# One inverse of softmax sums for two pairs of heads in the first batch of an attention and gated-MLP kernel

## The chip, the core and the metric

The kernel runs on one core of one Trainium2 chip. The metric is the time of one execution on the device, in microseconds (us); lower is better. The engines are named as in the profile: PE multiplies matrices (PEld is its weight load), DVE, ACT and POOL work on tiles elementwise, SP issues most of the DMAs. Each engine takes its instructions in the order in which the program lists them for that engine.

## The reference

Windowed attention with a bias that falls with distance, and then a gated MLP whose gate mixes along the sequence. Cut to what is computed:

```python
# attention: B, H, S, D = 8, 8, 576, 64; window 128
scores = q @ k.T / sqrt(D) + slope[h] * -abs(i - j)   # where 0 <= i - j < 128, else -1e9
attn = exp(scores - max(scores))
attn = attn / (sum(attn) + 1e-9)
x = attn @ v                                          # heads side by side: (8, 576, 512)
# gated MLP
h = relu(x @ w_in); u, v = h[..., :512], h[..., 512:]
v_n = (v - mean(v)) / sqrt(var(v) + 1e-6)
out = (u * (w_spatial @ v_n + b_spatial)) @ w_out
```

## The kernel before, in words

The work of a batch is attention for four pairs of heads, and then the units of the MLP: v (lines 696 to 722, and 724 to 750 for the rest of 64 rows), u (752 to 768), s (770 to 798) and o (800 to 822). Queries go in five tiles of 128 rows, t = 0 to 4, the last of 64. A tile of queries sees at most 256 keys.

Most batches go through `scores` and `attention`: the probabilities are split into two half-precision parts (line 576 on ACT, line 581 on DVE) and turned by a DMA transpose. The whole first batch, and pair 0 of the second, go through `raw_tile` instead (line 427), one call for each tile t and pair p. One call plans these steps, for both heads j of the pair:

- line 441, PE: the scores of both heads, into two of four PSUM buffers "s".
- line 447, DVE, once per head: bias and mask are added, the row minimum of the negated scores is kept in `rstat`, column NM, and the result goes to `prob[j]`, slot p.
- line 452, ACT, once per head: exp, with the sum of the row kept in `rstat`, column SM.
- lines 456 and 457, DVE: 1e-9 is added to the two sums, and the inverse is taken. Both instructions work on 128 x 2 elements: one column per head. The rest of this document calls the two together one inverse.
- lines 460 or 461: the probabilities are multiplied by the inverse, on ACT or on DVE, once per head.
- line 470, PE: the probabilities are transposed into a PSUM buffer "m" (of two, which the weight splits and the MLP units also use, in a fixed sequence).
- line 278: they are copied to SBUF (`pq`), on ACT or DVE; line 488, PE: they multiply v, into a buffer "x"; lines 278 and 496: the result is split into a high and a low part, `xt`, which the MLP reads.

`rstat` has eight rows of eight columns; tile t of pair p has row p + 4 (t mod 2), so that the rows of neighbouring tiles of t don't meet. A slot of `prob` is taken again by tile t + 1 of its pair, after the transposes of tile t. The calls stand in `first(t)` (line 844): the four pairs of one t, then the split of one quarter of the u weights (`split_w64`, lines 290 to 339, mostly DVE). `gated(0, ...)` calls `first(0)` and `first(1)`, and then `first(i + 2)` ahead of each v unit i.

What sets the order of the work: nothing is emitted at once. `plan.add` notes an operation with its engine, a cost in ns, a due time and the parts of buffers it reads and writes; `plan.order` (line 93) then plays the whole program through with these costs and emits, on each engine, the ready operation with the earliest due time. An operation added with `plan.either` goes to the engine on which it would end first, so the choice between lines 460 and 461 hangs on the plan. An inverse costs 190 in the plan, is due 900 after its tile, and a tile of pair p is due 1500 after that of pair p - 1. Which instruction stands behind which on DVE and ACT is so decided before the program runs, by modelled times:

```python
raw_tile(0, p, t, *loads[p], x0[p], p, 2000 + t * 6500 + p * 1500)   # line 846
plan.add("DVE", 190, due + 900, f, [(rstat, row)], [(rstat, row)])   # line 458
```

Of the kernel before, what the change touches and what calls it, by code (L numbers as in the profile page):

```python
# [16 lines left out]
ALU = mybir.AluOpType  # L17
# [123 lines left out]
def attn_gmlp_kernel(ctx, tc, qk, v, w_in, w_spT, b_sp, w_out, outT):  # L141
# [3 lines left out]
    nc = tc.nc  # L145
    B, H, D, _, S = qk.shape
    P = 2 * D
    NP = H // 2
    NQ = (S + P - 1) // P
# [29 lines left out]
    plan = Plan()  # L179
# [4 lines left out]
    def fixed(shape, dtype, name):  # L184
        t = const.tile(shape, dtype, name=name)
        return Buf(lambda: t)

    def dve(n, fast=False):
        return 75 + n / (1.92 if fast else 0.96)

    def act(n, pointers=0):
        return 95 + n / 1.2 + 93 * pointers
# [18 lines left out]
    r1 = fixed([P, S], F32R, "r1")  # L211
# [4 lines left out]
    prob = [fixed([P, NB * P], F32, f"prob{j}") for j in range(2)]  # L216
# [3 lines left out]
    rstat = fixed([P, 8, 8], F32, "rstat")  # L220

    def parts(b, a, z, step=P, key=()):

        return [(b, (*key, k)) for k in range(a // step, -(-z // step))]
# [122 lines left out]
    def win_weights(half, c, due, st):  # L347
        cs = slice(half * DH, (half + 1) * DH)
        split_w64((st, DH), (win, (half, c)), [plan.buf(work, "gs", 5, [P, DH], F32) for _ in range(2)],
                  lambda: win()[:, c, 0, cs], lambda: win()[:, c, 1, cs], due, WPE[half])  # L350
# [61 lines left out]
    def load(b, p, due, pieces, qtag=("qkraw", 3), vtag=("vraw", 3)):  # L412

        raw = plan.buf(work, *qtag, [P, 2, S], F32)
        vr = plan.buf(work, *vtag, [P, NQ, P], F32)
        src = qk[b, 2 * p:2 * p + 2].rearrange("h d a s -> (h d) a s")
        t0 = 0
        for i, t1 in enumerate(pieces):
            cs, ts_ = slice(t0 * P, min(S, t1 * P)), slice(t0, t1)
            plan.add("SP", dma(P * 2 * (cs.stop - cs.start) * 4), due[i], lambda cs=cs: nc.sync.dma_start(raw()[:, :, cs], src[:, :, cs]),  # L420
                     (), [(raw, t) for t in range(t0, t1)])
            plan.add("SP", dma(P * (t1 - t0) * P * 4), due[i] + 500, lambda ts_=ts_: nc.sync.dma_start(vr()[:, ts_], v[b, p][:, ts_]),
                     (), [(vr, t) for t in range(t0, t1)])
            t0 = t1
        return raw, vr

    def raw_tile(b, p, t, raw, vr, xt, slot, due):

        m, k0, k1 = min(P, S - t * P), max(0, (t - 1) * P), min(S, (t + 1) * P)
        n, c0 = k1 - k0, P if t == 0 else 0  # L430
        blocks = [(k, min(P, k1 - k)) for k in range(k0, k1, P)]
        row, NM, SM, TM, RC = (slot + 4 * (t % 2)) % 8, 0, 2, 4, 6
        st = lambda k, j: rstat()[:m, row, k + j:k + j + 1]
        sc = [plan.buf(ps, "s", 4, [P, 2, 2 * P], F32) for _ in range(2)]
        pr = [lambda j=j: prob[j]()[:m, slot * 2 * P:slot * 2 * P + n] for j in range(2)]
        cols = [parts(prob[j], slot * 2 * P, slot * 2 * P + n) for j in range(2)]

        def f():
            for j in range(2):
                rows = slice(j * D, (j + 1) * D)  # L440
                nc.tensor.matmul(sc[j]()[:m, 0, :n], raw()[rows, 0, t * P:t * P + m], raw()[rows, 1, k0:k1], start=True, stop=True)
        plan.add("PE", SWITCH // 2 + pe(*[4 * n]), due, f, [(raw, k) for k in range(k0 // P, t + 1)], [(sc[j], 0) for j in range(2)])
        for j in range(2):
            h = 2 * p + j

            def f(j=j, h=h):
                nc.vector.tensor_tensor_reduce(pr[j](), sc[j]()[:m, 0, :n], tabs[h]()[:m, c0:c0 + n], -0.125, 3e38,
                                               ALU.add, ALU.min, st(NM, j))
            plan.add("DVE", dve(n), due + 300, f, [(sc[j], 0), (tabs[h], 0)], cols[j] + [(rstat, row)])

            def f(j=j):
                nc.scalar.activation(pr[j](), pr[j](), AF.Exp, bias=st(NM, j), scale=-1.0, accum_out=st(SM, j))
            plan.add("ACT", act(n, 2), due + 600, f, cols[j] + [(rstat, row)], cols[j] + [(rstat, row)])

        def f():
            nc.vector.tensor_scalar(rstat()[:m, row, TM:TM + 2], rstat()[:m, row, SM:SM + 2], 1e-9, None, ALU.add)
            nc.vector.reciprocal(rstat()[:m, row, RC:RC + 2], rstat()[:m, row, TM:TM + 2])
        plan.add("DVE", 190, due + 900, f, [(rstat, row)], [(rstat, row)])
        for j in range(2):
            plan.either([("ACT", act(n, 1), lambda j=j: nc.scalar.activation(pr[j](), pr[j](), AF.Copy, scale=st(RC, j))),  # L460
                         ("DVE", dve(n, True), lambda j=j: nc.vector.tensor_scalar(pr[j](), pr[j](), st(RC, j), None, ALU.mult))],
# [83 lines left out]
    def scores(b, p):  # L545

        due = FIRST + b * PERIOD - LEAD - (NP - 1 - p) * PERIOD // 4
        st = stat[p % 2]
        SM, NM, RC, TM = range(4)
        raw, vr = load(b, p, [due - 12000], [NQ])  # L550
        RAWS, VRS = [(raw, t) for t in range(NQ)], [(vr, t) for t in range(NQ)]
        if (b, p) in RAW:
            xt = plan.buf(work, "xt", 6, [P, 2 * S + R], F32R)
            for t in range(NQ):
                raw_tile(b, p, t, raw, vr, xt, t % 4, due - 6000 + t * 1500)
            return lambda: xt
        for g, banks in enumerate((BANKS,) if b >= WHOLE else (BANKS[:2], ((BANKS[2][0], ("s", 4)),))):
            products(p, due, st, raw, RAWS, g, banks)
        pts = []
        for j in range(2):  # L560
            d = due + j * 1500

            def f(j=j):
                nc.vector.tensor_scalar(st()[:, TM, j, :NQ], st()[:, SM, j, :NQ], 1.0 / PSC, 1e-9 / PSC, ALU.mult, ALU.add)  # L564
            plan.add("DVE", 100, d, f, [(st, (SM, j, t)) for t in range(NQ)], [(st, (TM, j))])

            def f(j=j):
                nc.vector.reciprocal(st()[:, RC, j, :NQ], st()[:, TM, j, :NQ])  # L568
            plan.add("DVE", 120, d, f, [(st, (TM, j))], [(st, (RC, j))])
            for t in range(NQ):  # L570
                m = min(P, S - t * P)
                n = P if t == 0 else m + P
                cs = slice(OFF[t], OFF[t] + n)

                def f(j=j, t=t, m=m, cs=cs):
                    nc.scalar.activation(pq[j]()[:m, 0, cs], prob[j]()[:m, cs], AF.Copy, scale=st()[:m, RC, j, t:t + 1])  # L576
                cols, out = parts(prob[j], cs.start, cs.stop), [parts(pq[j], a * NB * P + cs.start, a * NB * P + cs.stop) for a in range(2)]
                plan.add("ACT", act(n, 1), d + 100 + t * 250, f, cols + [(st, (RC, j))], out[0])

                def f(j=j, t=t, m=m, cs=cs):  # L580
                    nc.vector.scalar_tensor_tensor(pq[j]()[:m, 1, cs], prob[j]()[:m, cs], st()[:m, RC, j, t:t + 1],  # L581
                                                   pq[j]()[:m, 0, cs], ALU.mult, ALU.subtract)
                plan.add("DVE", dve(n), d + 110 + t * 250, f, cols + [(st, (RC, j))] + out[0], out[1])
            pts.append(plan.buf(work, "pt", 3, [P, 2 * NB, P], F16))

            def f(j=j):
                nc.sync.dma_start_transpose(out=pts[j](), in_=pq[j]().rearrange("p a b -> p (a b)"))
            plan.add("SP", 3400, d + 1500, f, parts(pq[j], 0, 2 * NB * P), [(pts[j], 0)])

        return lambda: attention(p, due, vr, VRS, pts)  # L590
# [94 lines left out]
    def gated(b, xt, first=lambda t: None):  # L685
# [134 lines left out]
        for i in range(2):  # L820
            first(i)
        for i, t in enumerate(range(NQ) if b == 0 else VORDER):
            first(i + 2)
            v_rem() if t == NQ - 1 else v_unit(t)
# [16 lines left out]
    x0 = [plan.buf(work, "xt", 6, [P, 2 * S + R], F32R) for _ in range(NP)]  # L841
    loads = [load(0, p, [-50000 + 1000 * p, -20000 + 1000 * p], [2, NQ], *where[p]) for p in range(NP)]

    def first(t):
        for p in range(NP) if t < NQ else ():
            raw_tile(0, p, t, *loads[p], x0[p], p, 2000 + t * 6500 + p * 1500)
        if 0 <= t - 2 < NC_:
            c = t - 2
            win_weights(0, c, UDUE[c], w_u[c])
# [3 lines left out]
    def rest(b, p, f):  # L853
        xts.append(f())
        if p == NP - 1:
            gated(b, [xts.pop(0) for _ in range(NP)])

    gated(0, x0, first)
    todo = []
    for b in range(1, B):  # L860
        for p in range(NP):
            if b == 1 and (b, p) not in RAW and (b, p - 1) in RAW:
                clear()
            todo.append((b, p, scores(b, p)))
            if len(todo) > AHEAD:
                rest(*todo.pop(0))
# [35 lines left out]
```

## Time and profile before

| what | value |
|---|---|
| median of 3 runs | 634.85 us (632.7 to 635.41) |
| profiled execution | 634.76 us, of which 633.0 us are its span from first to last instruction |
| PE busy | 594.8 us (94% of the span) |
| PEld busy | 522.8 us (83%) |
| DVE busy | 537.0 us (85%), 1969 instructions |
| ACT busy | 425.7 us (67%) |
| POOL busy | 30.1 us (5%) |
| DMA | mean 127 GB/s |
| granted clock of PE, mean | 0.983 of full speed |

The shares are means over the whole span. The work of the first batch lies in the first 72 us, so the stretches of that time count here, each with the busy time of every engine and the granted clock of PE (1.00 is 2.4 GHz, 0.50 is 1.2 GHz). In lists of groups the columns are line, engine and operation, tiles, shapes and count, then busy us and mean ns of one, and the idle time of the engine ahead of them with what ended it. In timelines they are start, length, instruction, count, and in brackets the idle time ahead of it with its releaser. Neighbouring instructions of an engine overlap at their ends: what one costs its engine is the distance from its start to the next start.

### The profile page before, as it was taken

How to read it: one execution, taken by the hardware profiler on the slowest of the kernel's cores; microseconds unless marked ns; L12 is line 12 of the kernel's file. 1: busy time of each engine (PE TensorE's matmuls, PEld its weight loads, DVE VectorE, ACT ScalarE, POOL GpSimd, SP SyncE). 2: the span in 40 equal slices, each digit the busy share in tenths (PEclk: the TensorE clock that was granted, in tenths of full speed). 3: DMA queues.
4: the chain of work that ended last, by engine and by line, in shares of the span. 5: the costliest groups of instructions: out<-in, count | busy, mean ns of one | idle time of the engine just before them, and what ended most of it. 6: DMA issues, size and time to landing. Idle time of an engine off the chain costs nothing. (4 is left out here: it accounts for less than half of the span.)

```text
span 633.0 us, 14919 instructions
## 1 busy us (share of the span) xinstructions
PE 594.8 (94%) x5388; PEld 522.8 (83%) x5388; DVE 537.0 (85%) x1969; ACT 425.7 (67%) x1308; POOL 30.1 (5%) x53
## 2 busy tenths in 40 slices
PE   4888899799999899999999999999999999999997
PEld 2455578588789887999789988999899889998997
DVE  7999888889988979978899999999999899983632
ACT  4698675787767867858587676976597568752211
POOL 1000010000010001000110001000200010000100
PEclk9989799979999999999999999999999999999999
DMA  7902123498744873667636863597656761761001
GB/s 263 342 21 92 55 67 100 127 204 195 155 70 109 202 163 98 135 143 164 119 104 125 191 166 94 116 189 179 137 115 145 175 127 27 106 137 38 0 20 57
DMA packets 153613, 80.27 MB, mean 127 GB/s; under 512 B 132930, under 2 KB 144194, under 8 KB 153540
## 3 DMA queue, kind: packets, MB, share of 16 engines
q1 hardware_dynamic: 153540, 79.32, 53.4%
q8 instruction: 42, 0.69, 0.4%
q14 instruction: 31, 0.25, 0.1%
HBM read 37.13 MB, written 9.44 MB: 74 GB/s over the span
## 5 line engine op out<-in xcount | busy, mean ns | idle before, releaser
L541 ACT ACTIVATE prob<-prob,stat 128x256 f32<-128x256 f32 (+2 forms) x270 | 125.9, 469 | 36.7 <-DVE stat L535 36.5
L781 PE MATMUL m<-wsp,vn 128*128 128x288 f32 x768 | 122.0, 298 | 2.8 <-DVE o L278 1.6
L760 PE MATMUL m<-xt,win 128*128 128x288 f32 x768 | 111.3, 298 | 4.2 <-DVE u L283 2.3
L807 PE MATMUL m<-gs,wout 128*128 128x288 f32 x768 | 113.0, 302 | 0.7 <-DVE o L278 0.4
L781 PEld LDWEIGHTS m<-wsp,vn 128*128 128x128 f32 x768 | 107.2, 188 | 6.4 <-issue 2.0
L760 PEld LDWEIGHTS m<-xt,win 128*128 128x128 f32 x768 | 104.0, 188 | 9.0 <-DVE u L283 4.1
L807 PEld LDWEIGHTS m<-gs,wout 128*128 128x128 f32 x768 | 105.0, 191 | 6.2 <-DVE gs L795 1.8
L576 ACT ACTIVATE pq<-prob,stat 128x128 f16<-128x128 f32 x270 | 105.4, 468 | 5.0 <-DVE stat L568 1.6
L581 DVE SCALAR_TENSOR_TENSOR pq<-prob,stat,pq 128x128 f16<-128x128 f32 x270 | 105.0, 435 | 1.7 <-ACT pq L576 1.0
L708 PE MATMUL m<-win,xt 128*128 128x512 f32 x384 | 92.8, 396 | 1.7 <-ACT o L278 0.6
L708 PEld LDWEIGHTS m<-win,xt 128*128 128x128 f32 x384 | 72.2, 190 | 18.8 <-ACT vt L282 0.9
L535 DVE CUSTOM_DVE_ANT_0 prob<-s,tab 128x256 f32<-128x256 f32 (+2 forms) x222 | 74.8, 379 | 0.9 <-PE s L524 0.2
L789 DVE TENSOR_TENSOR u<-m,u 128x288 f32<-128x288 f32 x64 | 28.8, 451 | 28.8 <-PE m L781 28.5
L678 POOL TENSOR_TENSOR st<-st,nhalf 128x1 f32<-128x1 f32 (+1 forms) x40 | 26.1, 653 | 546.5 <-DVE st L674 526.4
L541 ACT ACTIVATION_READ_ACCUMULATOR prob<-prob,stat 128x1 f32 (+1 forms) x270 | 51.3, 190 | 0.0
L524 PE MATMUL s<-qkraw 64*64 64x192 f32 (+2 forms) x876 | 42.6, 317 | 5.0 <-DVE stat L535 5.0
L643 PE MATMUL x<-pt,vh 128*64 128x32 f16 (+6 forms) x756 | 42.4, 229 | 1.7 <-DMA pt<-pq 1.7
L524 PEld LDWEIGHTS s<-qkraw 64*64 64x64 f32 x876 | 31.4, 136 | 11.7 <-DVE stat L535 7.0
L643 PEld LDWEIGHTS <-vh 128*64 128x64 f16 x756 | 32.6, 110 | 7.0 <-issue 6.6
L669 DVE BATCH_NORM_STATS2 st<-vt 128x6 f32<-128x512 f32 (+1 forms) x40 | 27.5, 688 | 12.8 <-ACT vt L282 12.7
L278 ACT COPY o<-m 128x288 f32<-128x288 f32 x35 | 13.8, 393 | 35.9 <-PE m L807 25.7
L282 ACT ACTIVATE vt<-m 128x512 f32<-128x512 f32 x32 | 19.0, 595 | 26.7 <-DVE st L673 16.8
(133 smaller groups left out, 850.1 us busy)
## 6 DMA issues: line engine op xcount, KB each, us to landing
qkraw<-in_qk_dram SPq DMA_DIRECT2D x28, 576.0 KB, 4.1
out_dram<-o SPq DMA_DIRECT2D x64, 144.0 KB, 2.3
vraw<-in_v_dram SPq DMA_DIRECT2D x28, 320.0 KB, 3.1
vn<-in_w_in_dram SPq DMA_DIRECT2D x6, 512.0 KB, 6.5
pt<-in_w_out_dram SPq DMA_DIRECT2D x4, 512.0 KB, 4.2
gs<-in_w_spT_dram SPq DMA_DIRECT2D x4, 288.0 KB, 5.2
xt<-in_w_in_dram SPq DMA_DIRECT2D x2, 512.0 KB, 6.4
qkraw<-in_qk_dram SPq DMA_DIRECT2D x3, 320.0 KB, 8.7
```

Source lines behind the costliest of these rows:

```text
L524: nc.tensor.matmul(sc[k][j]()[out, i, a - k0:z - k0], raw()[rows, 0, q:q + D], raw()[rows, 1, a:z], start=True, stop=True, skip_group_chec ...
L535: nc.vector.tensor_tensor_reduce(pt(), sc()[:m, i, :n], tabs[h]()[:m, c0:c0 + n], -0.125, 3e38, ALU.add, ALU.min, st()[:m, NM, j, t:t + 1])
L541: nc.scalar.activation(pt(), pt(), AF.Exp, bias=st()[:m, NM, j, t:t + 1], scale=-1.0, accum_out=st()[:m, SM, j, t:t + 1])
L576: nc.scalar.activation(pq[j]()[:m, 0, cs], prob[j]()[:m, cs], AF.Copy, scale=st()[:m, RC, j, t:t + 1])
L581: nc.vector.scalar_tensor_tensor(pq[j]()[:m, 1, cs], prob[j]()[:m, cs], st()[:m, RC, j, t:t + 1], pq[j]()[:m, 0, cs], ALU.mult, ALU.subtract)
L643: nc.tensor.matmul(xp()[j * D:(j + 1) * D, x0:x0 + n], l()[:, kt, j * D:(j + 1) * D], rhs[:, o:o + n], start=j not in seen, stop=False, sk ...
L669: nc.vector.bn_stats(st()[:m, 0:6], vt()[:m])
L708: nc.tensor.matmul(pt(), xt[c]()[:, X0[a] + t * P:X0[a] + (t + 1) * P], win()[:, c, w, DH:DF], start=(n == 0), stop=(n == 3 * NC_ - 1))
L760: nc.tensor.matmul(pt()[:, :HS], win()[:, c, w, d * P:(d + 1) * P], xt[c]()[:, X0[a] + hf * HS:X0[a] + (hf + 1) * HS], start=(n == 0), sto ...
L781: nc.tensor.matmul(pt()[:, :HS], l, r, start=(n == 0), stop=(n == len(ops) - 1))
L789: nc.vector.tensor_tensor(u(), pt()[:, :HS], u(), ALU.mult)
L807: nc.tensor.matmul(pt()[:, :HS], wout()[:, d, w, e * P:(e + 1) * P], gs[d]()[:, a, :], start=(n == 0), stop=(n == 3 * ND - 1))
```

## The change

In the first batch two calls of `raw_tile`, for pairs 0 and 1 and for pairs 2 and 3 of one t, share one inverse. The rows of the two pairs in `rstat` are neighbours, and lines 456 and 457 work on 128 x 2 x 2 elements. The first call plans no inverse; the second plans one with its own due time, which reads and writes both rows. `raw_tile` is cut in two: up to the inverse, and `raw_rest`, from the multiplication on. In the first batch the first halves of both pairs are planned, and then both second halves. Pair 0 of the second batch has one inverse for each tile as before.

```diff
-    def raw_tile(b, p, t, raw, vr, xt, slot, due):
+    def raw_tile(b, p, t, raw, vr, xt, slot, due, sums=None):
...
-        def f():
-            nc.vector.tensor_scalar(rstat()[:m, row, TM:TM + 2], rstat()[:m, row, SM:SM + 2], 1e-9, None, ALU.add)
-            nc.vector.reciprocal(rstat()[:m, row, RC:RC + 2], rstat()[:m, row, TM:TM + 2])
-        plan.add("DVE", 190, due + 900, f, [(rstat, row)], [(rstat, row)])
+        r0, r1 = sums or (row, row + 1)
+
+        def f():
+            nc.vector.tensor_scalar(rstat()[:m, r0:r1, TM:TM + 2], rstat()[:m, r0:r1, SM:SM + 2], 1e-9, None, ALU.add)
+            nc.vector.reciprocal(rstat()[:m, r0:r1, RC:RC + 2], rstat()[:m, r0:r1, TM:TM + 2])
+        if sums is None or row == r1 - 1:
+            plan.add("DVE", 190, due + 900, f, [(rstat, r) for r in range(r0, r1)], [(rstat, r) for r in range(r0, r1)])
+        return lambda: raw_rest(b, p, t, raw, vr, xt, slot, due, row)
+
+    def raw_rest(b, p, t, raw, vr, xt, slot, due, row):
...
-                raw_tile(b, p, t, raw, vr, xt, t % 4, due - 6000 + t * 1500)
+                raw_tile(b, p, t, raw, vr, xt, t % 4, due - 6000 + t * 1500)()
...
     def first(t):
-        for p in range(NP) if t < NQ else ():
-            raw_tile(0, p, t, *loads[p], x0[p], p, 2000 + t * 6500 + p * 1500)
+        for p0 in range(0, NP, 2) if t < NQ else ():
+            r0 = p0 + 4 * (t % 2)
+            for f in [raw_tile(0, p, t, *loads[p], x0[p], p, 2000 + t * 6500 + p * 1500, (r0, r0 + 2)) for p in (p0, p0 + 1)]:
+                f()
```

## Rows read from the trace of the kernel before

**Rows 1.** Stretches of the span: busy us (instructions) of each engine, PEclk, DMA, GB/s.
```profile
core 0: us, PE busy (x) PEld busy (x) DVE busy (x) ACT busy (x) POOL busy (x), PEclk, DMA share, GB/s
13.00:24.00 11.00, 8.31 (x18) 3.42 (x18) 10.35 (x24) 4.80 (x9) 0.00 (x0) 1.00 1.06 388
24.00:72.00 48.00, 38.88 (x293) 25.34 (x291) 46.53 (x192) 41.38 (x127) 1.22 (x2) 0.96 0.32 102
72.00:80.00 8.00, 7.93 (x26) 5.07 (x27) 5.87 (x20) 4.35 (x15) 0.00 (x0) 0.57 0.01 2
80.00:116.00 36.00, 35.98 (x292) 30.39 (x294) 30.45 (x102) 22.60 (x61) 3.24 (x5) 1.00 0.31 95
116.00:132.00 16.00, 10.62 (x94) 8.73 (x86) 15.38 (x64) 13.38 (x49) 0.00 (x0) 0.74 0.67 153
132.00:633.00 501.00, 486.96 (x4655) 446.14 (x4653) 419.19 (x1522) 333.23 (x1033) 22.66 (x35) 1.00 0.57 124
```
**Rows 2.** Groups of instructions, DVE, 0 to 70 us: the inverses, shapes apart.
```profile
L457 DVE RECIPROCAL rstat<-rstat 128x2 f32<-128x2 f32 x16 | 2.7, 166 | 0.5
L456 DVE TENSOR_SCALAR rstat<-rstat 128x2 f32<-128x2 f32 x16 | 2.6, 164 | 1.2 <-ACT prob L452 1.2
...
L457 DVE RECIPROCAL rstat<-rstat 64x2 f32<-64x2 f32 x4 | 0.6, 157 | 0.1
L456 DVE TENSOR_SCALAR rstat<-rstat 64x2 f32<-64x2 f32 x4 | 0.6, 152 | 0.0
```
**Rows 3.** Timeline of DVE: one inverse of t = 1 and what follows it.
```profile
27.61 0.17 DVE L456 TENSOR_SCALAR rstat<-rstat 128x2 f32<-128x2 f32 x1
27.81 0.17 DVE L457 RECIPROCAL rstat<-rstat 128x2 f32<-128x2 f32 x1
27.89 0.41 DVE L447 CUSTOM_DVE_ANT_0 prob<-s,tab 128x256 f32<-128x256 f32 x1
```
**Rows 4.** Groups, DVE, whole span: the same two operations of other batches, on five columns.
```profile
L568 DVE RECIPROCAL stat<-stat 128x5 f32<-128x5 f32 x54 | 9.8, 185 | 0.9
L564 DVE TENSOR_SCALAR stat<-stat 128x5 f32<-128x5 f32 x54 | 8.6, 163 | 6.8 <-ACT prob L541 6.2
```
**Rows 5.** Timeline of DVE, t = 0: the last three of its four inverses.
```profile
9.08 0.17 DVE L456 TENSOR_SCALAR rstat<-rstat 128x2 f32<-128x2 f32 x1 [0.32 <-ACT prob L452]
...
10.74 0.17 DVE L456 TENSOR_SCALAR rstat<-rstat 128x2 f32<-128x2 f32 x1 [0.36 <-ACT prob L452]
...
12.40 0.17 DVE L456 TENSOR_SCALAR rstat<-rstat 128x2 f32<-128x2 f32 x1 [0.56 <-ACT prob L452]
```
**Rows 6.** Who waited for whom, DVE, 0 to 80 us: us in total, times, longest.
```profile
DVE rstat L456 <- ACT prob L452: 2.8, 4, 1.5
```
**Rows 7.** Timeline of DVE, t = 2: the inverses of pairs 2 and 3.
```profile
38.02 0.15 DVE L456 TENSOR_SCALAR rstat<-rstat 128x2 f32<-128x2 f32 x1
...
43.45 0.16 DVE L456 TENSOR_SCALAR rstat<-rstat 128x2 f32<-128x2 f32 x1
```
**Rows 8.** Timeline of PE, 72 to 87 us.
```profile
72.07 0.53 PE L470 MATMUL s<-ident,prob 128*128 128x128 f32 x2 [0.99 <-DVE prob L461]
...
77.23 3.91 PE L708 MATMUL m<-win,xt 128*128 128x512 f32 x12
...
84.25 2.91 PE L708 MATMUL m<-win,xt 128*128 128x512 f32 x12
```
**Rows 9.** Who waited for whom, PE, 24 to 72 us: us in total, times, longest.
```profile
PE x L488 <- DVE pq L278: 4.1, 4, 1.8
PE m L470 <- DVE prob L461: 1.0, 2, 0.5
```

More of the change, by code (lines that the diff above doesn't have):

```diff
@@ L453, in raw_tile @@
             plan.add("ACT", act(n, 2), due + 600, f, cols[j] + [(rstat, row)], cols[j] + [(rstat, row)])
+        r0, r1 = sums or (row, row + 1)
         def f():
-            nc.vector.tensor_scalar(rstat()[:m, row, TM:TM + 2], rstat()[:m, row, SM:SM + 2], 1e-9, None, ALU.add)
-            nc.vector.reciprocal(rstat()[:m, row, RC:RC + 2], rstat()[:m, row, TM:TM + 2])
-        plan.add("DVE", 190, due + 900, f, [(rstat, row)], [(rstat, row)])
+            nc.vector.tensor_scalar(rstat()[:m, r0:r1, TM:TM + 2], rstat()[:m, r0:r1, SM:SM + 2], 1e-9, None, ALU.add)
[4 more added lines that the diff above has]
+    def raw_rest(b, p, t, raw, vr, xt, slot, due, row):
+        m, k0, k1 = min(P, S - t * P), max(0, (t - 1) * P), min(S, (t + 1) * P)
+        n = k1 - k0
+        blocks = [(k, min(P, k1 - k)) for k in range(k0, k1, P)]
+        RC = 6
+        st = lambda k, j: rstat()[:m, row, k + j:k + j + 1]
+        pr = [lambda j=j: prob[j]()[:m, slot * 2 * P:slot * 2 * P + n] for j in range(2)]
+        cols = [parts(prob[j], slot * 2 * P, slot * 2 * P + n) for j in range(2)]
         for j in range(2):
```

## The prediction

> **What bounds the kernel now.** I read the stretches of the span first, because the page's means (PE 94%, DVE 85%) hide that the first batch has another limit than the rest [rows 1]. From 24 to 72 us, where tiles t = 1 to 4 of the first batch run, DVE is busy 46.53 of 48 us, ACT 41.38 and PE only 38.88. From 13 to 24 us, where the v weights are split, DVE has 10.35 of 11. So up to 72 us DVE sets the pace. From 72 us on PE does: 7.93 of 8 and then 35.98 of 36 us. From 116 to 132 us it is DVE once more (15.38 of 16), and after that PE to the end (486.96 of 501). A microsecond of DVE saved before 72 us can therefore reach the end if PE's full stretch begins earlier, and if nothing behind it gives it back.
>
> The second view are the waits. PE's waits between 24 and 72 us name DVE: 4.1 us for copies of probabilities to SBUF, 1.0 for scaled probabilities [rows 9]. DVE's own waits for the sums that an inverse needs are few: 2.8 us in four times, the longest 1.5 [rows 6]; three of them are in t = 0 (0.32, 0.36 and 0.56, together 1.24) [rows 5], so the fourth, the 1.5, lies outside t = 0. It can't lie in t = 1 to 4 either: the list of inverses up to 70 us has only 1.2 us of such waits, all used up by t = 0 [rows 2]. In t = 1 to 4 DVE never stands for an exp.
>
> **What goes.** The first batch has 20 inverses before 70 us, 16 on 128 rows and 4 on 64 [rows 2]. Ten remain. By their lengths (164 + 166 ns) ten would be 3.3 us, but lengths overlap. The timeline shows starts at 27.61, 27.81 and 27.89: an inverse takes 0.28 us from DVE, 0.20 for the addition, whose result the reciprocal needs, and 0.08 for the reciprocal, behind which an unrelated instruction starts at once [rows 3]. I take 0.28, since it is a distance between starts; ten are 2.8 us. The ends are 3.3 above, and below the two 0.08 of a pair that waits for nothing, 10 x 0.16 = 1.6 us.
>
> The Trainium skill (Vector Engine (DVE) Microarchitecture Reference, section 5.2) gives about 75 ns per instruction beyond its columns once neighbours overlap. By that, twenty instructions would be an estimated 1.5 us and the time about 633.3 us; the 0.08 of the reciprocal agrees, the 0.20 ahead of a dependent one doesn't.
>
> **What gets larger.** The ten that remain work on four columns. On two they take 164 and 166 ns, on five 163 and 185 [rows 2, 4]. Between them I take 10 ns, 0.1 us over all; the ends are 0 and 0.2.
>
> **What moves: t = 0.** Two of the ten savings, 0.56 us, are here. But DVE waits for ACT ahead of three of the four inverses [rows 5], so the last exp, not DVE, sets the time at which the last inverse can start, 12.40 us. In the new order the multiplications of pair 2 stand behind that point too, instead of at 11.15 us, after its own inverse. I count zero for t = 0: the saving against two scalings moved behind the last exp. The ends are a gain of 0.56 and a loss of the same size, since DVE may stand where those scalings were.
>
> **What moves: t = 1 to 4.** Eight savings, 8 x 0.28 = 2.24, less 0.1, is 2.1 us. The first pair of each two now waits for the exps of the second. That delays its scaling, transposes, copies and products; on the tile that I looked at, the inverses of pairs 2 and 3 of t = 2 are 43.45 - 38.02 = 5.4 us apart [rows 7], so pair 2 would come up to that much later. I cost this delay at nothing for DVE: the plan lists on DVE whatever is ready, and between 24 and 72 us it has other work, the splits of the u weights, the spatial weights and the next scores. If this cover fails, it is the rival below. Scalings may also change between ACT and DVE; ACT has 6.6 us free of 48 [rows 1], so this costs nothing either. No DMA is added or moved past another; the loads of the second batch follow the last scores of the first, and come earlier with them.
>
> **Sum.** 634.76 us (the profiled execution, 1.76 above its span of 633.0, and 0.09 below the median) less 2.1 gives 632.66; I say 632.6 us, 0.35% below the median. About 0.5%, 3.2 us, is what a measurement of this kernel can tell from no change.
>
> **Rivals.**
>
> *PE keeps its clock after 72 us.* PE idles 0.99 us at 72 us, waiting for DVE, and then runs at a granted clock of 0.57 for 8 us: between 1.2 and 2.4 GHz, mostly the lower [rows 1, 8]. The same twelve matmuls take 3.91 us there and 2.91 us at 84 us. A mean of 0.57 over 8 us is 8 x 0.43 / 0.5 = 6.9 us at the lower level, half of which, 3.4 us, is lost. PE is the bound there, so this counts in full. If a DVE with less to do feeds PE more evenly between 68 and 72 us, the drop goes: 632.6 - 3.4 = 629.2 us. For it: the wait ahead of it is for DVE. Against: two pairs' tiles now arrive together, which makes PE's work come in larger lumps with holes between. It could as well drop twice. Chance 0.28.
>
> *DVE stands at the shared inverses (slower).* DVE's order is fixed by a plan with modelled times. If on the chip the second pair's exps end later than planned, the shared inverse stands at the head of DVE's queue, and the scores, copies and splits behind it wait, with PE behind those. DVE has no spare time there [rows 1]. The waits that the trace shows run from 0.32 to 1.5 us [rows 5, 6]; at their middle, 0.9, ten are 9.1 us, less the 1.24 that stood in t = 0 before and the 2.8 saved: +5.1, or 639.8 us. It decides from a mean of (2.8 + 1.24 + 3.2) / 10 = 0.72 us for each. Against it: in t = 1 to 4 DVE stands at none of sixteen inverses, and the shared one needs no more than the second of two would have needed in its place. Chance 0.14.
>
> The Trainium skill (PSUM — Partial Sum Buffer, section "Engine vs sequencer instructions") says that VectorE's queue is strict FIFO, so nothing overtakes a waiting inverse; this is the rule that speaks against the change. The trace agrees as far as t = 0 goes: nothing of DVE runs in the 0.56 us ahead of the inverse at 12.40 [rows 5].
>
> *The gain is given back.* From 116 to 132 us DVE is full again, with PE at 10.62 of 16 us and a clock of 0.74 [rows 1]. If the second batch's softmax is listed otherwise there, or its loads don't come earlier, PE's earlier start ends in a longer hole: 634.8 us. Chance 0.15.
>
> That the change would not do what it says is no rival: the halving follows from the loops.
>
> **How the numbers follow.** My forecast has 0.43, the clock rival 0.28, the gain given back 0.15, the standing DVE 0.14. The forecast's own range is 631.5 (ten times 0.33 us saved, 3.3) to 634.2 (eight times 0.16, less 0.2 for the columns and 0.56 lost in t = 0: 0.5 saved). The range of 8 in 10 reaches from 628.5, the clock rival with more saved, to 638.0, which takes in the gain given back and the standing DVE up to 0.7 us for each inverse. Faster by over 0.5%, below 631.7: the 0.28 of the clock rival and 0.06 of my forecast, at the upper end of the saving, together 0.34. Slower: 0.13 of the 0.14 of the standing DVE. The same: 0.53.
>
> **What would show it.** Right: ten instructions fewer of each of lines 456 and 457 in the first 70 us, each on 128 x 4 elements and about as long as before; DVE still full from 24 us on; the first u unit about 2 us earlier, and so the end. The clock rival shows as 1.00 in the stretch where the third v unit runs. The standing DVE shows as waits of line 456 for line 452 of more than 7 us. The gain given back shows as an earlier third v unit with the same end. The prediction is wrong if DVE has 2 us less work by 72 us and PE's full stretch does not begin earlier, or if the time leaves 628.5 to 638.0.

## The result, and the profile after

The changed kernel takes 626.17 us (median; 624.92 to 626.95), the kernel before 634.07 in the same comparison (four runs of each): a ratio of 0.9871, 95% interval 0.985 to 0.9892. That is 7.9 us faster, outside the predicted range of 628.5 to 638.0, and nearly four times the 2.1 us of the forecast.

The stretches of the span of the changed kernel, columns as in [rows 1]:

```profile
24.00:72.00 48.00, 40.68 (x296) 26.28 (x296) 45.54 (x175) 40.77 (x132) 1.49 (x2) 0.92 0.32 101
72.00:80.00 8.00, 8.00 (x32) 5.07 (x30) 5.73 (x17) 3.66 (x11) 0.00 (x0) 0.63 0.00 1
80.00:116.00 36.00, 36.00 (x301) 31.09 (x302) 31.70 (x106) 23.97 (x69) 3.41 (x5) 1.00 0.27 89
116.00:132.00 16.00, 11.91 (x108) 10.14 (x100) 15.48 (x61) 13.89 (x48) 0.00 (x0) 0.89 0.77 189
```

Against [rows 1] little has changed up to 116 us. DVE is still full from 24 to 72 us (45.54 of 48, before 46.53), and PE still runs at a lowered clock from 72 to 80 us (0.63, before 0.57). From 116 to 132 us PE does 1.3 us more at a higher clock.

The inverses themselves, groups of DVE from 0 to 70 us, the waits of DVE up to 80 us, and the timeline of DVE around the first shared inverse of t = 1:

```profile
L459 DVE RECIPROCAL rstat<-rstat 128x4 f32<-128x4 f32 x8 | 1.4, 179 | 0.3
L458 DVE TENSOR_SCALAR rstat<-rstat 128x4 f32<-128x4 f32 x8 | 1.3, 164 | 1.3 <-ACT prob L452 1.3
...
```
```profile
DVE rstat L458 <- ACT prob L452: 2.8, 3, 1.5
```
```profile
28.18 0.17 DVE L458 TENSOR_SCALAR rstat<-rstat 128x4 f32<-128x4 f32 x1
28.38 0.18 DVE L459 RECIPROCAL rstat<-rstat 128x4 f32<-128x4 f32 x1
28.48 0.26 DVE L509 TENSOR_TENSOR xt<-x,xt 128x128 fp32r<-128x128 f32 x1
```

There are ten (eight here, and two on 64 rows), with 164 and 179 ns where [rows 2] have 164 and 166. From start to the next instruction's start one takes 0.30 us (28.18 to 28.48), against 0.28 in [rows 3]. DVE stands for sums as long as before, 2.8 us [rows 6], and of that 1.3 us lies before 70 us, where [rows 2] had 1.2.

The same stretch of DVE's work in both kernels, from the first copy of t = 0 (24.36 and 24.00 us) to the first inverse of the second batch (71.21 and 69.92), first the kernel before, then the changed one:

```profile
24.36:71.21 46.85, 38.56 (x290) 25.26 (x290) 45.77 (x187) 40.37 (x126) 1.22 (x2) 0.96 0.32 102
24.00:69.92 45.92, 39.50 (x290) 25.58 (x290) 43.49 (x167) 39.01 (x125) 1.49 (x2) 0.93 0.33 106
```

DVE works 2.28 us less (43.49 for 45.77) but takes only 0.93 us less (45.92 for 46.85), because it stands 2.43 us instead of 1.08. Three new waits make 1.28 us of that: 0.20 for PE at 42.53, 0.62 for ACT at 45.04 and 0.46 for PE at 46.93. The timeline of the kernel before shows no such wait in this stretch.

PE ahead of 72 us and its third v unit, from the timeline of PE:

```profile
70.82 0.44 PE L483 MATMUL s<-ident,prob 128*128 128x128 f32 x2 [1.29 <-ACT prob L473]
...
75.89 3.90 PE L721 MATMUL m<-win,xt 128*128 128x512 f32 x12
```

The third v unit starts at 75.89, before at 77.23 [rows 8]: 1.3 us earlier, where the forecast had 2.1. So at 76 us only 1.3 of the 7.9 us are there. Where do the other 6.6 come from? Over the whole span PE is busy 594.8 us before and 591.6 after, and stands 38.2 and 33.6 us. The rest unit of the v half runs once in each batch on PE, so it can serve as a milestone. From its start in the first batch to its start in the fourth, and from there to the fifth, kernel before and changed kernel:

```profile
87.00:306.10 219.10, 207.16 (x1996) 185.24 (x1995) 192.10 (x718) 161.90 (x504) 9.14 (x14) 0.98 0.61 138
306.10:375.10 69.00, 67.74 (x674) 62.10 (x673) 63.02 (x235) 50.03 (x159) 3.48 (x5) 1.00 0.61 142
```
```profile
85.70:300.80 215.10, 203.86 (x1996) 183.24 (x1995) 193.51 (x718) 160.31 (x504) 8.81 (x14) 0.99 0.62 140
300.80:368.40 67.60, 67.23 (x674) 61.89 (x673) 63.91 (x237) 50.31 (x161) 3.25 (x5) 1.00 0.65 145
```

Both kernels do the same work in them (1996 and 674 instructions of PE), after the first batch's attention is over, and the changed kernel is 4.0 and 1.4 us faster there; about 1 us more comes behind them. The first gain is mostly PE busy for 3.3 us less, with a higher mean clock (PE stands 11.24 us there, before 11.94); the second is PE standing for 0.37 us instead of 1.26. The clock differs most from 110 to 140 us, before and after:

```profile
110.00:140.00 30.00, 24.60 (x231) 20.87 (x224) 26.05 (x119) 23.46 (x83) 0.21 (x1) 0.83 0.66 159
110.00:140.00 30.00, 25.36 (x256) 21.69 (x249) 28.16 (x125) 25.74 (x92) 0.50 (x2) 0.94 0.76 167
```

An estimate from these rows: 30 x (0.94 - 0.83) = 3.3 us of PE's full speed, as much as PE is busy less. These are two single executions.

The instructions of those batches are the same ones, but their sequence is not. The plan plays the whole program through, and a different first batch leaves another state behind; so every engine's list differs for some batches. Then the lists settle: from some row on, row n of PE's 5890 rows equals row n + 768, one batch further, and DVE's and ACT's lists repeat likewise. In the kernel before this begins at PE's row 2475, in the fourth batch; in the changed kernel at row 1707, in the third. And all kernels of this document settle into the same lists: from PE's row 2475 on (306 us in the kernel before) PE's lists are equal row for row, and so are the last 848 rows of DVE's (from about 338 us). Whatever the lists do, they do it ahead of that.

### The profile page after: what moved, and what is told of

It is laid out like the page before. It is cut to its first block, busy times and chain, and to the rows that moved or that the text cites. A ratio compares the mean times of both kernels' runs of the same rounds, so it can differ in the third digit from the quotient of the medians.

```text
span 625.2 us, 14903 instructions
## 1 busy us (share of the span) xinstructions
PE 591.6 (95%) x5388; PEld 521.6 (83%) x5388; DVE 536.7 (86%) x1945; ACT 422.7 (68%) x1312; POOL 30.0 (5%) x53
## 5 line engine op out<-in xcount | busy, mean ns | idle before, releaser
L820 PE MATMUL m<-gs,wout 128*128 128x288 f32 x768 | 110.3, 299 | 0.2 <-ACT o L278 0.2
L820 PEld LDWEIGHTS m<-gs,wout 128*128 128x128 f32 x768 | 103.5, 189 | 4.1 <-DVE gs L808 1.5
L656 PE MATMUL x<-pt,vh 128*64 128x256 f16 (+6 forms) x756 | 42.0, 229 | 0.0
L656 PE MATMUL x<-pt,vl 128*64 128x256 f16 (+6 forms) x378 | 35.5, 228 | 0.0
```

What stands on the lines that cost most here:

```text
L656: nc.tensor.matmul(xp()[j * D:(j + 1) * D, x0:x0 + n], l()[:, kt, j * D:(j + 1) * D], rhs[:, o:o + n], start=j not in seen, stop=False, sk ...
L820: nc.tensor.matmul(pt()[:, :HS], wout()[:, d, w, e * P:(e + 1) * P], gs[d]()[:, a, :], start=(n == 0), stop=(n == 3 * ND - 1))
```

## The experiments

A shared inverse can act in two ways: by the time it saves on DVE (theory B), or by the lists that the plan makes with it (theory A). Planning the two pairs' tiles together is not a way of its own: with the second halves behind both first halves, but an inverse for each pair, the plan lists every engine instruction for instruction as before. What re-lists the program is that one inverse waits for both pairs, here at the cost of one.

**Same lists, other DVE time.** Two kernels hold the lists fixed. In the first the changed kernel issues each shared inverse as two:

```diff
-            nc.vector.tensor_scalar(rstat()[:m, r0:r1, TM:TM + 2], ...)
-            nc.vector.reciprocal(rstat()[:m, r0:r1, RC:RC + 2], ...)
+            one = lambda r: (nc.vector.tensor_scalar(rstat()[:m, r, TM:TM + 2], ...), nc.vector.reciprocal(rstat()[:m, r, RC:RC + 2], ...))
+            [one(r) for r in range(r0, r1)]
```

> The changed kernel with every engine's list as it is there, except that each shared inverse on DVE is issued as two, one for each pair: 20 DVE instructions more, about 2.8 us of DVE. Theory A, the order (most of the 7.9 us comes from the new lists of all engines, the saved DVE time is worth at most 2.8): 626.2 to 629.0 us. Theory B, the saved DVE time (what DVE does less before 72 us grows on its way through later stretches): back near the kernel before, 632 to 634.

In the second the kernel before leaves ten out:

```diff
-            nc.vector.tensor_scalar(rstat()[:m, row, TM:TM + 2], ...)
-            nc.vector.reciprocal(rstat()[:m, row, RC:RC + 2], ...)
+            if b or p % 2: nc.vector.tensor_scalar(rstat()[:m, row, TM:TM + 2], ...)
+            if b or p % 2: nc.vector.reciprocal(rstat()[:m, row, RC:RC + 2], ...)
```

> The kernel before with every engine's list as it was, except that the inverses of pairs 0 and 2 of the first batch are left out (their probabilities are multiplied by whatever stands in rstat): 20 DVE instructions less. Theory A, the order: 631.3 to 634, a gain of 0 to 2.8 us. Theory B, the saved DVE time: near the changed kernel, 626 to 628.

Measured: 0.9903 (0.9882 to 0.9924) with the new lists and all 20 inverses, and 0.9959 (0.9945 to 0.9974) with the old lists and ten. So the lists alone bring 1.0%, 6.1 us, and the ten inverses 0.3 to 0.4% (0.9903 to 0.9871, 2.0 us; 1 to 0.9959, 2.6 us). Theory B falls as the main cause; the two parts add up. The 6.1 us are clear of noise. The 2.0 us are hardly so (the intervals of 0.9903 and 0.9871 touch), the 2.6 us are.

**Same instructions, other costs in the plan.**

```diff
-        plan.add("DVE", 190, due + 900, f, [(rstat, row)], [(rstat, row)])
+        plan.add("DVE", 95 if b == 0 else 190, due + 900, f, [(rstat, row)], [(rstat, row)])
```

> The kernel before with the same operations, but the plan counts an inverse of the first batch as 95 instead of 190, so the lists come out somewhat differently (about 100 of 1971 DVE instructions move). No DVE time is saved. Theory A, in the form that any new list shifts the time by several us: away from 634.1 by more than 2 us, either way. Theory A, in the form that only what the shared inverse does to the lists counts, and theory B: 633 to 635.

```diff
-            plan.add("DVE", 190, due + 900, f, ...)
+            plan.add("DVE", 190 * (r1 - r0), due + 900, f, ...)
```

> The changed kernel with the same operations, but the plan counts a shared inverse as 380 instead of 190, so the plan's DVE time is that of before; about 280 DVE instructions move. Theory A, if any new list shifts the time by several us: away from 626.2 by more than 2 us. Theory A, if the pairing itself makes the good list, and theory B: 625 to 628.

Measured: 0.9958 (0.9944 to 0.9971) for the kernel before with a cost of 95, so 0.4% (2.5 us) comes and goes with a number that no engine ever sees. That is the outcome of the form in which any new list shifts the time. The changed kernel with 380 has 0.9859 (0.9833 to 0.9885), which its interval can't tell from the changed kernel's 0.9871: here 280 moved instructions shift nothing that can be seen.

**Old and new lists in one program.** Four kernels plan twice, once with an inverse for each pair and once with shared ones, issue the first plan's operations up to a mark, and then the rest in the sequence of the second plan. All were meant to have 20 inverses. Where the new plan is issued, `swaps` names the inverse of the first pair, which that plan doesn't hold, and it is issued with the second.

```diff
+        a, b = runs["new"], runs["old"]
+        at = next((i for i, (n, _) in enumerate(a) if n == self.marks.get("u0")), len(a))
+        done = {n for n, _ in a[:at]}
...
+        for n, fn in a[:at] + [x for x in b if x[0] not in done]:
+            if n in swaps and ("new" == ("new" if n in done else "old")):
+                full[swaps[n]][0][0][2]()
             fn()
```

> Each pair has its own inverse (20, the DVE work of before). Until the first u unit of the first batch the engines' lists are those of the changed kernel, from there on the plan of the kernel before lists what is left. Ends of the scale: 633.9 us (old lists all through) and 627.6 (new lists all through, 20 inverses). Theory A1, the gain lies in how the first batch itself is listed: about 627.6. Theory A2, it lies in what the plan lists afterwards: about 633.9.

> The reverse, 20 inverses too: the lists of the kernel before until the first u unit of the first batch, those of the changed kernel from there on. Theory A1: about 633.9. Theory A2: about 627.6.

> As the last, but the lists change only at the first v unit of the second batch (160 us), 20 inverses. Theory A2a, the gain lies in the stretch from 87 to 160 us, where the MLP of the first batch meets the softmax of the second: about 633.9. Theory A2b, it lies in the lists of the later batches, which repeat from batch to batch one batch earlier in the changed kernel: about 627.6.

> The lists of the changed kernel until the first v unit of the second batch, those of the kernel before from there on, 20 inverses. Theory A1 and A2a: about 627.6. Theory A2b: about 633.9.

Measured: new then old 1.0007 (0.9994 to 1.002) with the mark at the first u unit, and 1.0 (0.9985 to 1.0015) with the mark at 160 us. Old then new 0.9909 (0.9883 to 0.9935) and 0.9925 (0.9901 to 0.9949). The two new-then-old kernels don't have 20 inverses but 30, whatever their expectations say: the ten that `swaps` issued are not noted in `done`, and so stand a second time at the head of the rest. DVE at the joint of the last kernel, and the first of PE's waits in it from 164 to 377 us:

```profile
159.43 0.16 DVE L486 TENSOR_SCALAR rstat<-rstat 128x2 f32<-128x2 f32 x1
...
162.00 0.16 DVE L487 RECIPROCAL rstat<-rstat 64x2 f32<-64x2 f32 x1
```
```profile
PE m L753 <- ACT vt L310: 3.5, 1, 3.5
```

The repeated inverses hold DVE for 2.65 us, to 162.08. From 155 to 175 us PE is busy 15.03 of 20 us at a granted clock of 0.83, where the kernel before has 19.52 at 1.00. In the kernel with the mark at the first u unit they run from 86.27 to 88.98, and PE stands 1.19 and 1.46 us right behind. So these two kernels lose at the joint much of what new lists could have gained ahead of it, and their 1.0007 and 1.0 speak neither for theory A2 nor against A1.

Old then new has 20 inverses and none twice. New lists all through had 0.9903, and new lists behind 160 us alone 0.9925: about three quarters of the gain ((1 - 0.9925) / (1 - 0.9903) = 0.77) can be had there, when the first batch's attention is over. The share is loose, since the intervals are 0.5 to 1.0% of 0.8 to 1.2%. What new lists bring ahead of 160 us stays open. In the traces the changed kernel is well ahead by then: the rest unit of its second batch starts at 157.05 us, that of the kernel before at 164.44. Some 1.6 us of this are no lead (an estimate: 18 of a batch's 768 rows of PE's list, at about 68 us for a batch, stand ahead of the unit in the kernel before and behind it in the changed one), and 3.3 us are the clock from 110 to 140 us. The last old-then-new kernel, whose PE list is the old one up to row 1133, has 0.89 in that stretch and the kernel before 0.83, so the lists alone don't set this clock.

**When the lists repeat.** This led to theory C: the batches until the lists repeat cost more than those after, because PE waits more in them. The row at which they repeat is known before a kernel runs, so it can be put to the test with kernels whose row alone was known. The cost in the plan chooses it:

```diff
-        plan.add("DVE", 190, due + 900, f, [(rstat, row)], [(rstat, row)])
+        plan.add("DVE", (200 if b == 0 else 190), due + 900, f, [(rstat, row)], [(rstat, row)])
```

> The kernel before with the same operations and 20 inverses, but the plan counts an inverse of the first batch as 200 instead of 190. From some batch on the lists of all engines repeat from batch to batch: in the kernel before from the fourth batch on (row 2475 of PE's 5890), in the changed kernel from the third (row 1707), and with 200 from the second (row 927). Theory C, the earlier the lists repeat, the less PE waits in the batches between: about 0.988 to 0.992 of before. Theory R, the gain needs the shared inverse, by its DVE time or by the pairs' tiles going together: 0.997 to 1.003.

> The same with a cost of 180: about 390 DVE instructions are listed elsewhere, but the lists repeat from the fourth batch on, as in the kernel before. Theory C: 0.994 to 1.002 of before. If any other list is as good as the new one (the kernel before has an unlucky list): about 0.990.

And the change itself with a cost at which the lists repeat late:

```diff
-            plan.add("DVE", 190, due + 900, f, ...)
+            plan.add("DVE", (95 if sums else 190), due + 900, f, ...)
```

> The changed kernel with its ten shared inverses, counted in the plan as 95 instead of 190: the lists then repeat only from the fourth batch on, as in the kernel before. Theory C: the saved DVE time alone, 0.994 to 0.998 of before. Theory R: as the changed kernel, 0.985 to 0.989.

Measured: 0.9884 (0.9853 to 0.9914) with 200, 0.9957 (0.994 to 0.9974) with 180, and 0.9942 (0.9922 to 0.9963) for the change with 95. All three fall where theory C put them. The kernel before with one cost changed from 190 to 200, and not an instruction saved, is as fast as the changed kernel within the intervals; the changed kernel with late lists keeps only what its ten inverses save.

The same two stretches in the kernel with 200, and the first of them in the one with 180:

```profile
88.30:300.80 212.50, 204.65 (x1995) 184.21 (x1995) 193.25 (x716) 158.02 (x499) 9.73 (x14) 0.98 0.63 142
300.80:368.40 67.60, 67.24 (x673) 61.89 (x672) 63.80 (x237) 50.29 (x161) 3.24 (x5) 1.00 0.65 145
```
```profile
87.90:304.40 216.50, 207.22 (x1995) 183.75 (x1994) 194.50 (x723) 157.49 (x496) 10.11 (x14) 0.98 0.61 139
```

All kernels but the last of this section, by the batch from which the lists repeat (each stretch from one execution; the first stretch of new then old has the joint with its ten inverses in it):

| lists repeat from | kernels | ratio to before | first to fourth batch, us | next batch, us |
|---|---|---|---|---|
| fourth batch, row 2475 | before; cost 95; cost 180 | 1; 0.9958; 0.9957 | 219.1; 216.7; 216.5 | 69.0; 69.3; 68.7 |
| | ten left out; the change with cost 95 | 0.9959; 0.9942 | 218.5; 216.2 | 68.3; 68.3 |
| | new then old, both marks | 1.0007; 1.0 | 222.8; 221.8 | 68.3; 68.8 |
| third batch, row 1707 | the change; new lists with 20 inverses | 0.9871; 0.9903 | 215.1; 214.3 | 67.6; 67.6 |
| | old then new, both marks | 0.9909; 0.9925 | 215.1; 215.8 | 67.6; 67.6 |
| second batch, row 927 | cost 200; the change with cost 380 | 0.9884; 0.9859 | 212.5; 211.8 | 67.6; 67.5 |

The last two columns fall in steps with the first, with 68.3 to 69.3 us for the next batch where the lists repeat from the fourth batch, and 67.5 or 67.6 where they repeat earlier. PE's list is the same in all kernels in that batch; DVE's and ACT's differ in its first half. Lists that are equal don't make equal times, though: the two batches behind it, with the same lists in all kernels, take 67.6 to 68.1 and 68.0 to 69.5 us. And the ratios part only the fourth batch from the others: with 20 inverses 0.9957 and above against 0.9925 and below, with ten 0.9942 and above against 0.9871 and below. Within their intervals the second batch is no better than the third (0.9884 against 0.9903 with 20 inverses, 0.9859 against 0.9871 with ten).

What PE waits for from 160 to 380 us, in the kernel before, in the changed kernel and in the one with 200:

```profile
PE m L760 <- ACT vt L282: 1.9, 2, 1.4
PE m L781 <- DVE o L278: 1.6, 1, 1.6
PE x L643 <- DMA pt<-pq: 1.1, 1, 1.1
...
```
```profile
PE m L721 <- DVE vt L283: 1.7, 1, 1.7
...
```
```profile
PE m L760 <- DVE u L283: 1.7, 3, 0.7
PE m L708 <- ACT o L278: 1.2, 1, 1.2
PE m L760 <- ACT vt L282: 0.4, 1, 0.4
```

The first list goes on to 7.3 us in all, the second to 6.9; the third is whole and has 3.3. So fewer waits, as theory C has it, show with 200, whose lists repeat from the second batch: from the first batch's rest unit to the fourth's PE stands 7.85 us there, with 180 9.28 and before 11.94. In the changed kernel (11.24) they hardly show; its trace has less busy time of PE instead. That early repeating goes with a shorter time is shown; that fewer waits are the reason is not, beyond the trace of the kernel with 200.

**What an inverse costs.** The kernel with new lists and own inverses issues each of them twice. That makes 25 more, not 20: the five of pair 0 of the second batch are doubled too.

```diff
-            [one(r) for r in range(r0, r1)]
+            [one(r) for r in range(r0, r1) for _ in range(2)]
```

> The changed kernel's lists, each pair of heads with its own inverse and each inverse issued twice: 40 inverses instead of 10, 20 more than with one each. If the time of an inverse on DVE (0.28 us) counts in full, 20 x 0.28 = 5.6 us above the kernel with one for each pair: 0.999 of before. If half of it is covered, 0.995. If nothing counts, 0.990.

Measured: 1.0 (0.9985 to 1.0015), against 0.9903 with one each: 0.97%, 6.1 us (4.5 to 7.7) for 25, or 0.24 us each; 0.31 if the five of the second batch, which run from 78 us on, cost nothing. In the traces the third v unit of PE starts at 84.64 us instead of 76.98, so all of the loss is there before 85 us. Between 24 and 72 us nothing covers an inverse, as far as this interval tells; it counts in full.

## Why the prediction was wrong

**The direction was right, and the DVE term in its size.** The sum had 2.1 us for ten inverses; with the lists held fixed they measure 2.0 and 2.6, with wide intervals. The 0.28 us that were read from starts in the timeline came out as 0.24 to 0.31 when 25 were added. The page of the Trainium skill that was set against it there (Vector Engine (DVE) Microarchitecture Reference, section 5.2), with about 75 ns for an instruction, would make an estimated 0.15 of one inverse, less than this case measures. The 10 ns for four columns are 13 in the trace (179 against 166 ns). For t = 0 the forecast took nothing: the first product of the weight split on PE (line 333) starts 0.36 us earlier (14.60, before 14.96), but the kernel with new lists and 20 inverses has 14.41, so this can't be told from nothing.

**The step that failed** is the one that took everything behind the first batch as given: "A microsecond of DVE saved before 72 us can therefore reach the end if PE's full stretch begins earlier, and if nothing behind it gives it back." The sum had one term for DVE and none for the lists of the later batches, though the text knew that a plan makes them from modelled costs. Another listing appeared in it only as a way to lose ("listed otherwise there"), from 116 to 132 us, and was given no price of its own either way. The runs put 6.1 us on exactly this, and lists that change only behind 160 us bring about three quarters of it. An inverse that waits for two pairs changes the state that the first batch leaves behind, and the lists settle one batch sooner (two, when it costs twice 190 in the plan). Nothing in the trace of the kernel before told the sign: a cost of 200 brings as much as the change, one of 180 does not.

**A second step failed, and is worth less.** The delay of the first pair was costed "at nothing for DVE". In t = 1 to 4 DVE worked 2.28 us less, about what was forecast (2.1), but it stood 1.35 us more, mostly at the three new waits between 42 and 47 us. The kernel with new lists and 20 inverses has the same three (0.20, 0.36 and 0.46 us), so they come with the new lists. This is why PE's third v unit began 1.3 us earlier and not 2.1.

**The rivals.** PE did not keep its clock after 72 us: the granted clock is 0.63 there, 0.57 before, and PE stands 1.29 us ahead of it, longer than the 0.99 of [rows 8]. DVE does not stand at the shared inverses: 1.3 us before 70 us, all of it in t = 0. The Trainium skill's rule on the strict FIFO (PSUM — Partial Sum Buffer, section "Engine vs sequencer instructions") so had nothing to hold up; in t = 1 to 4 the second pair's sums were there in time. The gain was not given back from 116 to 132 us: PE does 1.3 us more there than before.

**What stays open.** Why the plan's lists settle in the second, third or fourth batch, how much of the gain lies ahead of 160 us, and which single instruction of a list that is not settled costs PE most: the last was read from the waits and not tried. The kernel before is also 0.4% slower than two others whose lists repeat as late (0.9958 and 0.9957), so the row at which they repeat is not all. And in the two traces part of the gain between the first and the fourth batch is PE's clock (busy 3.3 us less in the same work), which was not held fixed by itself. Over a whole execution it is not the cause: at a mean clock of 0.986 the kernel before took 631.9 to 634.8 us and the changed kernel 625.6 and 626.7.

## What to carry to other kernels

Where a program's order comes from a plan with modelled costs, any change to one operation's cost or inputs re-lists what follows, and the re-listing can be worth several times the operation: here 6.1 against 2.0 us. Price the two apart, by kernels with the lists of one and the instructions of the other, before a gain is put down to the instructions. And run the old instructions under a few neighbouring costs: costs of 180, 190 and 200 alone gave 0.9957, 1 and 0.9884, so 190 was the worst of three, and a new cost gets what a new operation seemed to bring.

## What was not expected of the hardware

One thing: on a DVE that is busy 95% of the time or more (45.84 of 48 us with new lists and 20 inverses), a pair of instructions on two columns costs 0.24 to 0.31 us at the end of the program, 500 us later, through stretches in which PE is the bound. Nothing between the first batch and the end took it back: in the two traces the added pairs cost 7.7 us at the third v unit and 7.5 us at the end (633.8 against 626.3).
